# Spreading the gathers of mirrored rows over the steps, ordering the one-channel loads, and giving four side copies their own buffers

## The chip, the cores and the metric

The kernel runs on one core of a Trainium2 chip. The metric is device time of one execution in microseconds (us); smaller is better. Every quoted median is that of the fast runs of one kernel, with its lowest and highest run in brackets. Names of engines: PE is TensorE (matmuls), DVE is VectorE, ACT is ScalarE, POOL is GpSimd, SP is SyncE, whose queue issues most of the DMAs here.

## The reference

The input x has shape (8, 3008, 256) in float32: eight batches, a sequence of 3008 rows, 256 channels. The reference takes the real part of a two-dimensional Fourier transform, and feeds every row to a small network with an unusual activation.

```python
X = np.fft.fft(x, axis=1)            # over the 3008 rows
X = np.fft.fft(X, axis=2)            # over the 256 channels
x = X.real.reshape(8 * 3008, 256)
h = x @ w_in                          # 256 -> 2048
g = h * np.cos(h)
out = g @ w_out                       # 2048 -> 256
```

## The kernel before

The kernel uses the mirror symmetry of the transform, so that it handles 12032 columns instead of 24064 rows. It works in 47 tiles of 256 columns, each tile in 8 steps: 376 steps. A step is twenty 128x256 float32 matmuls, about 4.75 us of PE. Every step also asks four block sums of POOL (`sum_1` to `sum_4`), which feed matmuls into the accumulators pB, pC and pD.

Work for the next batch is scattered among these steps. POOL adds and subtracts rows with their mirror images ("folds", two halves of 1.0 us each); to this end, the rows must lie in four buffers `L[0]` to `L[3]`. The unmirrored ones come by plain DMAs from SP; the mirrored ones come by four indirect DMAs (gathers) that POOL issues itself:

```python
def load_x(b):
    L = [spool.tile([128, 6 * ND], FP, tag=f"xl{j}", bufs=1, name=f"xl{j}") for j in range(4)]
    for j in (2, 1):
        runs = (...)                               # two pieces of each row buffer
        for c, part in runs:
            nc.gpsimd.indirect_dma_start(          # not pinned: the scheduler places it
                out=L[j][:, part], out_offset=None, in_=xflat,
                in_offset=bass.IndirectOffsetOnAxis(ap=ix[:, c : c + 1], axis=0),
                element_offset=b * SEQ * ND,
            )
    for j, row in ((0, 0), (3, HALF)):
        nc.sync.dma_start(...)                     # plain loads
    ...
```

One channel (number 128) does not fit the symmetric layout of the channels. Its values are loaded for all batches at the start, one element at a time (four loads of 8 x 768 elements), stored to memory, read back in another layout by twelve small reads, folded by POOL, transformed by 28 matmuls, copied from PSUM by ACT ("side copies"), combined by DVE (first half) and POOL (second half), stored, and broadcast to the table `Rb`, which ACT needs for the third tile.

```python
def load_ext(j):                                   # called for j = 0..3
    ...
    with nc.allow_non_contiguous_dma(reason="one channel"):
        if j == 1:
            copy(0, 1, 0, 1)
            copy(1, 768, SEQ - 1, -1)
        else:
            copy(0, 768, (0, SEQ, HALF, HALF)[j], -1 if j == 2 else 1)
    nc.sync.dma_start(out=xe_dr[j], in_=t[:, 0:768])

def ext_side(g):                                   # called for g = 0..3
    par = g % 2
    t = spool.tile([128, 2 * NH], FP, tag=f"xt{par}", bufs=1, name=f"xt{par}")
    ...
    act(t[0:NB, 0:n], state["ext"][32 * g : 32 * g + NB, 0:n])
    state["side", par] = t[0:NB]
...
for b in range(1, NB):
    s0 = (b - 1) * steps_b                         # steps_b = 47
    l0 = s0 - (8 if b > 1 else 1.5)
    at(l0 * T + 0.1, lambda b=b: state.update(L=load_x(b)))
```

`at(t, fn)` sorts pieces of the program by a planned time, and `T` is one step. The plan fixes the program order. An instruction that is pinned (`pin`, which stands for `tc.keep_in_program_order`) keeps that order on its engine; one that is not may be moved by the scheduler.

## Time and profile before

| | before |
|---|---|
| time, median of 3 runs given with the kernel | 1990.61 us (1987.91 to 1991.32) |
| span of the profiled execution | 1993.1 us |
| PE busy | 1940.6 us, 97% |
| DVE, ACT, POOL busy | 71%, 73%, 68% |
| PE not busy | 52.5 us |

First lines of the page of before (span and busy time of PE and POOL), and from its list of groups the block sums of POOL (count, then busy time and mean ns of one, then idle time ahead of them and who ended it):

```profile
span 1993.1 us, 28143 instructions
PE 1940.6 (97%) x8855; PEld 1654.5 (83%) x8855; DVE 1417.0 (71%) x2343; ACT 1452.1 (73%) x2790; POOL 1352.9 (68%) x1860
L265 POOL TENSOR_TENSOR G<-G 128x256 f32<-128x256 f32 x1504 | 1079.7, 729 | 585.4 <-DVE G L705 490.0
```

PE is the bottleneck, and only its 52.5 idle microseconds can be won. POOL is idle for hundreds of microseconds, mostly waiting for DVE, and that costs nothing by itself. What counts is where POOL is late for PE. The view of waits of before shows what PE waits for (us in total, number of waits, longest):

```profile
PE pB L256 <- POOL G L265: 13.2, 14, 2.5
PE H L256 <- ACT H L268: 7.6, 5, 3.7
PE H L256 <- POOL xe L265: 7.5, 1, 7.5
```

The first line is POOL's lateness with block sums; the third is one wait for the one-channel data.

**The gathers.** POOL's timeline of before at the gathers of batch 3 (start, duration, what, and in brackets the idle time ahead of it):

```profile
408.20 3.03 POOL L265 TENSOR_TENSOR G<-G 128x256 f32<-128x256 f32 x4 [1.31 <-PE H L256]
411.19 0.99 POOL L315 TENSOR_TENSOR o<-xl 128x381 f32<-128x381 f32 x1
412.45 0.99 POOL L162 DMA_INDIRECT xl<-in_x_dram,ix  x1 [0.27 <-POOL o L315]
413.75 0.95 POOL L162 DMA_INDIRECT xl<-in_x_dram,ix  x1 [0.30 <-issue]
414.71 3.03 POOL L265 TENSOR_TENSOR G<-G 128x256 f32<-128x256 f32 x4
```

Between two sets of four sums there are a fold and two gathers, so this set of sums starts 6.5 us after the last, where a step has 4.75. PE's timeline of before shows what comes of it, here in batch 5:

```profile
895.06 0.59 PE L256 MATMUL pB<-G,w 128*128 128x256 f32 x2
897.11 0.70 PE L256 MATMUL pB<-G,WT 128*128 128x256 f32 x2 [1.46 <-POOL G L265]
897.64 1.03 PE L256 MATMUL H<-Ir,Ws 127*128 127x256 f32 x4
...
906.28 0.59 PE L256 MATMUL pB<-G,w 128*128 128x256 f32 x2
907.52 0.70 PE L256 MATMUL pB<-G,WT 128*128 128x256 f32 x2 [0.64 <-POOL G L265]
908.06 1.03 PE L256 MATMUL H<-Ir,Ws 127*128 127x256 f32 x4
```

Two waits of 1.46 and 0.64 us stand in this batch.

**The one-channel data.** The timeline of SP's queue in before. A DMA's "duration" here is how long its issue occupied the queue:

```profile
37.22 32.23 SPq L527 DMA_DIRECT2D x<-in_x_dram  x4
69.55 18.00 SPq L542 DMA_DIRECT2D xe_dr<-x  x3
87.60 0.68 SPq L527 DMA_DIRECT2D x<-in_x_dram  x1
88.34 10.06 SPq L548 DMA_DIRECT2D xs<-xe_dr  x1
```

The fourth big load is issued only at 87.60, behind three stores. Windows of 2 us of before show the hole that this leaves: the last two numbers of a line are the busy share of the DMA engines and the GB/s moved (ahead of them busy time and count of PE, PE's weight loads, DVE, ACT, POOL, then PE's granted clock).

```profile
84.00:86.00 2.00, 2.00 (x11) 1.74 (x11) 1.29 (x2) 1.49 (x3) 1.84 (x3) 1.00 0.31 19
86.00:88.00 2.00, 2.00 (x11) 1.76 (x10) 1.22 (x3) 1.97 (x5) 1.65 (x4) 1.00 0.00 0
```

The last of the twelve reads was issued by 108.4 us. POOL then folds, and PE goes on after its longest wait (POOL's line, then PE's, from their timelines in before):

```profile
110.50 0.38 POOL L265 TENSOR_TENSOR xs<-xs 128x96 f32<-128x96 f32 x1 [8.29 <-DMA out_dram<-ot]
```

```profile
111.30 4.18 PE L256 MATMUL H<-MC,xe 128*8 128x189 f32 x28 [7.48 <-POOL xe L265]
```

**The side copies.** ACT's timeline of before: the third and fourth copy wait for DVE, which still reads the two buffers that hold the first and second:

```profile
124.62 0.48 ACT L268 ACTIVATE xt<-H 8x378 f32<-8x378 f32 x1 [1.71 <-DVE ab L262]
125.72 0.48 ACT L268 ACTIVATE xt<-H 8x376 f32<-8x376 f32 x1 [0.62 <-DVE rx L262]
```

### The profile page before, as it was taken

The numbers are of one execution on the slowest core, as the hardware profiler recorded it, in microseconds if no ns is written. First come the engines' busy times: TensorE is split into PE (matmuls) and PEld (weight loads), VectorE is DVE, ScalarE is ACT, GpSimd is POOL, SyncE is SP. The second block draws the span as 40 slices with busy tenths as digits, with TensorE's granted clock in tenths as the row PEclk, the third lists the DMA queues.
The fourth block names the chain that finished last, engine by engine and source line by source line (L and its number), as shares of the span: only waits on it lengthen the run. The fifth ranks groups of instructions, "written<-read, shape, count | busy, mean of one in ns | idle before, by whom it ended". The sixth has DMA issues, their size and how long they took to land.

```text
span 1993.1 us, 28143 instructions
## 1 busy us (share of the span) xinstructions
PE 1940.6 (97%) x8855; PEld 1654.5 (83%) x8855; DVE 1417.0 (71%) x2343; ACT 1452.1 (73%) x2790; POOL 1352.9 (68%) x1860
## 2 busy tenths in 40 slices
PE   7979999999999999999999999999999999999997
PEld 4858888888888888888888888888888888888886
DVE  4757767777677767776677776777777776677776
ACT  2757767777777777777777777777777777777775
POOL 4758748786577866777667875778757776555654
PEclk9989999999999999999999999999999999999999
DMA  9822100121011110021100301013010110001101
GB/s 295 4 30 60 43 13 19 31 61 24 12 19 44 46 28 11 18 58 32 26 18 12 84 8 24 11 21 88 7 19 11 27 23 9 14 12 17 16 12 22
DMA packets 260207, 66.17 MB, mean 33 GB/s; under 512 B 247186, under 2 KB 250026, under 8 KB 260058
## 3 DMA queue, kind: packets, MB, share of 16 engines
q1 hardware_dynamic: 256362, 51.77, 15.0%
q0 software_dynamic: 3696, 12.60, 2.1%
q8 instruction: 70, 1.15, 0.2%
q14 instruction: 79, 0.65, 0.1%
HBM read 39.49 MB, written 24.80 MB: 32 GB/s over the span
## 4 chain that ended last, share of the span: by engine, by line
PE 82%; DMA 4%; DVE 4%; POOL 4%; ACT 2%; issue 2%; SPq 2%; DVEq 0%; POOLq 0%
PE H L256 33%; PE pC L256 14%; PE pB L256 14%; PE pD L256 14%; PE pA L256 7%; DMA x<-in_x_dram 2%; POOL G L265 2%; DVE G L705 1%; ACT G L268 1%; SPq L527 1%; DVE G L262 1%; DMA pick<-pick_mats 1%; POOL xl L162 1%; DVE v L262 1%; DMA xl<-in_x_dram 1%
## 5 line engine op out<-in xcount | busy, mean ns | idle before, releaser
L265 POOL TENSOR_TENSOR G<-G 128x256 f32<-128x256 f32 x1504 | 1079.7, 729 | 585.4 <-DVE G L705 490.0
L705 DVE SCALAR_TENSOR_TENSOR G<-H,G 128x512 f32<-128x512 f32 x376 | 257.0, 683 | 283.7 <-ACT G L268 283.7
L262 DVE TENSOR_TENSOR G<-H,G 128x512 f32<-128x512 f32 x376 | 260.0, 692 | 222.8 <-ACT G L268 219.7
L268 ACT ACTIVATE G<-H 128x512 int32<-128x512 f32 x376 | 224.5, 597 | 241.2 <-DVE G L262 239.8
L256 PE MATMUL H<-Rr,Wc 128*128 128x256 f32 x1504 | 387.9, 380 | 7.6 <-ACT H L268 7.6
L256 PE MATMUL H<-Ir,Ws 127*128 127x256 f32 x1504 | 388.6, 380 | 1.4 <-ACT E L268 1.4
L256 PE MATMUL pC<-G,WT 128*128 128x256 f32 x1504 | 387.3, 379 | 1.7 <-DVE u L262 1.6
L268 ACT ACTIVATE H<-Rb,wex 128x256 f32<-128x256 f32 x752 | 360.1, 479 | 34.1 <-DVE G L705 10.4
L268 ACT ACTIVATE E<-H 128x512 f32<-128x512 f32 x376 | 224.2, 596 | 216.7 <-PE H L256 214.0
L256 PEld LDWEIGHTS H<-Rr,Wc 128*128 128x128 f32 x1504 | 284.3, 190 | 56.5 <-ACT H L268 10.4
L256 PEld LDWEIGHTS pC<-G,WT 128*128 128x128 f32 x1504 | 284.1, 189 | 45.0 <-PE H L256 5.1
L256 PEld LDWEIGHTS H<-Ir,Ws 127*128 127x128 f32 x1504 | 283.4, 190 | 45.2 <-ACT E L268 6.6
L268 ACT ACTIVATE G<-G,halfpi 128x512 f32<-128x512 f32 x376 | 269.4, 716 | 1.5 <-DVE G L262 1.5
L262 DVE TENSOR_TENSOR G<-E,H 128x512 f32<-128x512 f32 x376 | 255.0, 678 | 12.6 <-PE H L256 10.4
L262 DVE TENSOR_TENSOR M<-G,M 128x512 f32<-128x512 f32 x376 | 257.6, 685 | 0.0
L705 DVE SCALAR_TENSOR_TENSOR G<-G,M 128x512 f32<-128x512 f32 x376 | 254.1, 676 | 0.4 <-ACT M L268 0.3
L268 ACT ACTIVATE M<-M,halfpi 128x512 f32<-128x512 f32 x376 | 246.1, 655 | 0.4 <-DVE M L262 0.3
L256 PE MATMUL pB<-G,WT 128*128 128x256 f32 x752 | 227.9, 385 | 13.2 <-POOL G L265 13.2
L256 PE MATMUL pA<-G,w 128*128 128x256 f32 x752 | 223.8, 379 | 2.3 <-issue 2.3
L268 ACT ACTIVATE M<-G 128x512 int32<-128x512 f32 x376 | 224.4, 597 | 0.0
L256 PE MATMUL pB<-G,w 128*128 128x256 f32 x752 | 223.7, 379 | 0.0
L256 PE MATMUL pD<-G,w 128*128 128x256 f32 x752 | 223.7, 379 | 0.0
(125 smaller groups left out, 1786.2 us busy)
## 6 DMA issues: line engine op xcount, KB each, us to landing
out_dram<-ot SPq DMA_DIRECT2D x504, 32.0 KB
xl<-in_x_dram SPq DMA_DIRECT2D x16, 512.0 KB
xl<-in_x_dram SPq DMA_DIRECT2D x32, 128.0 KB
out_dram<-ot SPq DMA_DIRECT2D x256, 2.0 KB
MC<-dft_mats SPq DMA_DIRECT2D x4, 943.5 KB
Rb<-r SPq DMA_DIRECT2D x10, 376.0 KB
w<-in_moe_w_in_dram SPq DMA_DIRECT2D x4, 512.0 KB
w<-in_moe_w_out_dram SPq DMA_DIRECT2D x1, 2048.0 KB
```

Of the source, the lines that this page charges most:

```text
L162: nc.gpsimd.indirect_dma_start(out=L[j][:, part], out_offset=None, in_=xflat, in_offset=bass.IndirectOffsetOnAxis(ap=ix[:, c : c + 1], axi ...
L256: nc.tensor.matmul(out_, lhsT=lhsT, rhs=rhs, start=start, stop=stop, skip_group_check=True)
L262: pin(nc.vector.tensor_tensor(out=o, in0=a, in1=b, op=op))
L265: pin(nc.gpsimd.tensor_tensor(out=o, in0=a, in1=b, op=op))
L268: pin(nc.scalar.activation(out=o, in_=i, func=func, **kw))
L527: nc.sync.dma_start(out=t[:, s0:s1], in_=bass.AP(tensor=xt, offset=x.offset + row * ND + 128, ap=[[SEQ * ND, NB], [step * ND, s1 - s0], [1 ...
L705: nc.vector.scalar_tensor_tensor(out=o, in0=h, scalar=TWO_PI, in1=c, op0=ALU.mult, op1=ALU.mult)
```

## The change

The change has three parts. The first takes POOL's gathers out of the crowded steps: for batches 2 to 7 they are pinned one per step, behind the four block sums, in steps that have no fold. Batch 1's four are pinned as well, which puts them later than the scheduler had put them, and the last rows of batch 7 go through SP's queue. The second pins all DMAs of the one-channel data in a fixed order: row 0 (a single element per batch) first, the four big loads, four stores, twelve reads. The third gives the four side copies four buffers. PE, DVE and ACT get exactly the same instructions in the same order as before; only POOL's and SP's orders change.

```diff
-    def load_x(b):
+    def gather_x(b, L, j, short):
+        ...                                  # the same slices and indices as before
+        pin(
+            nc.gpsimd.indirect_dma_start(
+                out=L[j][:, part], ...
+            )
+        )
+    GATHERS = [(2, 0), (2, 1), (1, 0), (1, 1)]
+    def load_x(b, gather=True):
...
-        if b == NB - 1:
-            nc.gpsimd.dma_start(out=L[1][0:1, 2 * ND : 5 * ND], ...)
+    def last_rows(b, L):
+        nc.sync.dma_start(out=L[1][0:1, 2 * ND : 5 * ND], ...)
...
+    def spin(**kw):
+        pin(nc.sync.dma_start(**kw))
+    def load_ext():
+            copy(1, 0, 1, 0, 1)              # row 0
+            copy(0, 0, 768, 0, 1)
+            copy(1, 1, 768, SEQ - 1, -1)
+            copy(2, 0, 768, HALF, -1)
+            copy(3, 0, 768, HALF, 1)
             for j in range(4):
+                spin(out=xe_dr[j], in_=rows[j][:, 0:768])
+            for j in range(4):               # three reads each
+                spin(out=xs[:, j, :, 0:4], ...)
...
-            [128, 2 * NH], FP, tag=f"xt{par}", bufs=1, name=f"xt{par}"
+            [128, 2 * NH], FP, tag=f"xt{par}", bufs=2, name=f"xt{par}"
-        state["side", par] = t[0:NB]
+        state["side", g] = t[0:NB]
...
-        at(l0 * T + 0.1, lambda b=b: state.update(L=load_x(b)))
+        at(l0 * T + 0.1, lambda b=b: state.update(L=load_x(b, b == 1)))
+        if b > 1:
+            for n, (j, short) in enumerate(GATHERS):
+                at((l0 + n) * T + 1.3, lambda ...: gather_x(b, state["L"], j, short))
+        if b == NB - 1:
+            at((l0 + 3) * T + 1.4, lambda b=b: last_rows(b, state["L"]))
```

More of the change, by code (lines that the diff above doesn't have):

```diff
@@ L148 @@
     nc.sync.dma_start(out=ix, in_=IX_dr.ap())
-    def load_x(b):
+    def gather_x(b, L, j, short):
+        if short:
+            c, part = 2 * j - 1, slice(0, 2 * ND)
+        else:
+            c = 4 if j == 1 and b == NB - 1 else 2 * j - 2
+            part = slice(2 * ND, 6 * ND)
+        pin(
+            nc.gpsimd.indirect_dma_start(
+                out=L[j][:, part],
+                out_offset=None,
+                in_=xflat,
+                in_offset=bass.IndirectOffsetOnAxis(ap=ix[:, c : c + 1], axis=0),
+                element_offset=b * SEQ * ND,
+            )
+        )
+    GATHERS = [(2, 0), (2, 1), (1, 0), (1, 1)]
+    def load_x(b, gather=True):
         L = [
@@ L154, in load_x @@
         ]
-        for j in (2, 1):
-            runs = (
-                (4 if j == 1 and b == NB - 1 else 2 * j - 2, slice(2 * ND, 6 * ND)),
-                (2 * j - 1, slice(0, 2 * ND)),
-            )
-            for c, part in runs:
-                nc.gpsimd.indirect_dma_start(
-                    out=L[j][:, part],
-                    out_offset=None,
-                    in_=xflat,
-                    in_offset=bass.IndirectOffsetOnAxis(ap=ix[:, c : c + 1], axis=0),
-                    element_offset=b * SEQ * ND,
-                )
+        if gather:
+            for j, short in GATHERS:
+                gather_x(b, L, j, short)
         for j, row in ((0, 0), (3, HALF)):
@@ L177, in load_x @@
                 )
-        if b == NB - 1:
-            nc.gpsimd.dma_start(
-                out=L[1][0:1, 2 * ND : 5 * ND], in_=xrows(b, SEQ - 3, 1, 1, 3)
-            )
-        return L
+        return L
+    def last_rows(b, L):
+        nc.sync.dma_start(
+            out=L[1][0:1, 2 * ND : 5 * ND], in_=xrows(b, SEQ - 3, 1, 1, 3)
+        )
     CC = cpool.tile([128, 512], FP, tag="CC")
@@ L518, in minus_sum, with copy @@
                 )
-    def load_ext(j):
-        if j == 0:
-            state["x1"] = spool.tile([128, HALF + 1], FP, tag="rx", bufs=1, name="x1")
-        t = state["x1"][j * NB : (j + 1) * NB]
-        def copy(s0, s1, row, step):
-            nc.sync.dma_start(
-                out=t[:, s0:s1],
+    def spin(**kw):
+        pin(nc.sync.dma_start(**kw))
+    def load_ext():
+        x1 = spool.tile([128, HALF + 1], FP, tag="rx", bufs=1, name="x1")
+        xs = state["xs"] = spool.tile([128, 4, NB, 6], FP, tag="xs", bufs=1, name="xs")
+        rows = [x1[j * NB : (j + 1) * NB] for j in range(4)]
+        def copy(j, s0, s1, row, step):
+            spin(
+                out=rows[j][:, s0:s1],
                 in_=bass.AP(
@@ L534, in copy @@
             )
-        with nc.allow_non_contiguous_dma(reason="one channel"):
-            if j == 1:
-                copy(0, 1, 0, 1)
-                copy(1, 768, SEQ - 1, -1)
-            else:
-                copy(0, 768, (0, SEQ, HALF, HALF)[j], -1 if j == 2 else 1)
-        nc.sync.dma_start(out=xe_dr[j], in_=t[:, 0:768])
-    def get_ext():
-        xs = state["xs"] = spool.tile([128, 4, NB, 6], FP, tag="xs", bufs=1, name="xs")
-        with nc.allow_non_contiguous_dma(reason="runs of six"):
+        with nc.allow_non_contiguous_dma(reason="one channel, then runs of rows"):
+            copy(1, 0, 1, 0, 1)
[3 more added lines that the diff above has]
+            copy(3, 0, 768, HALF, 1)
             for j in range(4):
-                nc.sync.dma_start(
+                spin(out=xe_dr[j], in_=rows[j][:, 0:768])
+            for j in range(4):
+                spin(
                     out=xs[:, j, :, 0:4],
@@ L553, in get_ext @@
                 for h in range(2):
-                    nc.sync.dma_start(
-                        out=xs[64 * h : 64 * h + 64, j, :, 4:6], in_=pairs[h]
-                    )
+                    spin(out=xs[64 * h : 64 * h + 64, j, :, 4:6], in_=pairs[h])
     def fold_ext():
@@ L600, in ext_rows @@
             state["rx"] = rx[0:NB]
-        rx, uv, b = state["rx"], state["side", 0], state["side", 1]
+        rx, uv, b = state["rx"], state["side", 2 * kodd], state["side", 2 * kodd + 1]
         a = spool.tile([128, NE], FP, tag="ab", bufs=2, name="ab")[0:NB]
@@ L1048 @@
         at(t, fn)
-    for j in range(4):
-        at(-T, lambda j=j: load_ext(j))
-    at(8 * T, get_ext)
-    at(11 * T + 1.35, fold_ext)
-    at(11 * T + 2.905, clear_ext)
-    at(11 * T + 4.75, dft_ext)
-    at(12 * T + 1.46, lambda: ext_side(0))
-    at(12 * T + 1.47, lambda: ext_side(1))
-    at(13 * T + 1.0, lambda: ext_rows(0, vtt))
-    at(13 * T + 1.46, lambda: ext_side(2))
-    at(13 * T + 1.47, lambda: ext_side(3))
-    at(14 * T + 1.35, lambda: ext_rows(1, gtt))
-    at(14 * T + 2.0, lambda: spread_ext(0, 1))
+    at(-T, load_ext)
+    e0 = 11 * T
+    at(e0 + 1.35, fold_ext)
+    at(e0 + 2.905, clear_ext)
+    at(e0 + 4.75, dft_ext)
+    for g in range(4):
+        at(e0 + T * (1 + g // 2) + 1.46, lambda g=g: ext_side(g))
+    at(e0 + 2 * T + 1.0, lambda: ext_rows(0, vtt))
+    at(e0 + 3 * T + 1.35, lambda: ext_rows(1, gtt))
+    at(e0 + 3 * T + 2.0, lambda: spread_ext(0, 1))
     fold_keys = [(k, p) for k in FOLDS for p in range(2 if k[0] not in "czx" else 1)]
@@ L1066 @@
         l0 = s0 - (8 if b > 1 else 1.5)
-        at(l0 * T + 0.1, lambda b=b: state.update(L=load_x(b)))
+        at(l0 * T + 0.1, lambda b=b: state.update(L=load_x(b, b == 1)))
+        if b > 1:
+            for n, (j, short) in enumerate(GATHERS):
+                at(
+                    (l0 + n) * T + 1.3,
+                    lambda b=b, j=j, short=short: gather_x(b, state["L"], j, short),
+                )
+        if b == NB - 1:
+            at((l0 + 3) * T + 1.4, lambda b=b: last_rows(b, state["L"]))
         f0 = max(7, s0 - 1)
```

## The prediction

> **What bounds the kernel.** TensorE: the page gives it 1940.6 of 1993.1 us busy (97%); DVE, ACT and POOL have 68 to 73%. The timeline shows steps of twenty 128x256 matmuls, one per 4.75 us, mostly without a gap. Only the 52 us of PE idle time can be won. Windows of 10 us place it: about 16 us in the start (before 57 us), 12 us between 103 and 141 us, about 10 us around the gathers of batches 2 to 7, most of the rest at the end.
>
> **Gathers.** In before, the scheduler lifts each batch's four gathers to just behind the last reads of the old rows, two and two, among steps that also carry a fold. A gather holds POOL for 0.96 us plus 0.30 us before it. Such a step has 3.03 us of block sums and 1.0 us of fold: 0.7 us is free against 2.5 us for two gathers. The PE timeline shows pB waiting for POOL: 0.81 (batch 2), 0.64+0.65, 1.06+0.66, 1.46+0.64, 0.81+0.66, and 0.53+2.46 in batch 7, where POOL also waits 1.14 us for a gather to land. Sum 10.4 us. In after, the instruction order has one gather per step, in steps without folds, behind the fourth sum, where POOL idles 1.3 us and more for DVE anyway. The last rows go over the sync queue. I expect all these waits gone: -10.4 us.
>
> **One-channel loads.** Each big one is 6144 single elements; from 46 to 82 us the DMA is 0.9 busy at 2 GB/s. This agrees with the Trainium skill (DMA: Bandwidth & Descriptors, Rules for kernel authors): a strided last dimension makes one descriptor per element. In before the fourth is issued only after three stores (87.6 us); windows of 2 us show the DMA idle from 84 to 89 us. It lands at 102.8; then one store, nine small reads (5.3 us of issues) and 1.7 us to landing at 110.2. After: the fourth follows at once and, I estimate, lands at 99 us; but all twelve reads (7.0 us) come after its store, so they land near 108.3. The PE stall before the one-channel matmuls (7.5 us) shrinks by about 2 us. Row 0 first changes nothing.
>
> **Side copies in own buffers.** ACT waits 1.71+0.62 us for DVE before copies 2 and 3. But DVE is busy with the rows until 125.69, where its next product now starts at 126.84: only 1.15 us is gained, as POOL's rows and the broadcast (PE waits at 136.8 and 141.0) follow this chain: -1.2 us.
>
> **Start.** Batch 1's gathers move behind the wex load and two weight sums; wex may land 1 to 3 us earlier, and PE's 3.7 us wait at 40 us shrink. That gains nothing: PE only reaches the wait for the DMA-bound one-channel data sooner. PE, DVE and ACT keep their order exactly.
>
> **Sum.** 1990.6 - 10.4 - 2.0 - 1.2 = 1977.0 us; range 1971 to 1983. Faster by over 2%: 0.01; within 2%: 0.98; slower by over 2%: 0.01.
>
> **What would show it.** Waits of pB for POOL gone from batches 2 to 7; no DMA hole near 86 us; POOL's wait for the one-channel data ending near 108 instead of 110.2; ACT's waits before the side copies gone, the broadcast landing 3 us before 139.9.
>
> **What would make it wrong.** Gathers that hold POOL longer at the new place, or delay the next sums; reads issuing slower than 0.6 us each; a start so late that it, not the DMA, ends the stall.

## The result, and the profile after

| | before | after |
|---|---|---|
| median (lowest to highest) | 1990.96 us (4 runs, 1987.91 to 1991.63) | 1973.76 us (4 runs, 1972.83 to 1977.76) |
| span of the profiled execution | 1993.1 us | 1971.4 us |
| PE busy | 1940.6 us | 1938.6 us |
| PE not busy | 52.5 us | 32.8 us |

The ratio is 0.992, with a 95% interval of 0.9903 to 0.9938: a little faster, within 2%. Ratios are computed as the mean time of one kernel's fast runs over that of the other's in the same rounds, so they are not quite the ratios of the medians. The medians differ by 17.2 us, where 13.6 was predicted. Over all rounds together, before ran 37 times with a median of 1990.91 us (1985.72 to 2001.78) and after 10 times with 1974.18 us (1972.83 to 1982.77), so 16.7 us apart.

The same lines of the page, for after:

```profile
span 1971.4 us, 28146 instructions
PE 1938.6 (98%) x8855; PEld 1654.3 (84%) x8855; DVE 1416.1 (72%) x2343; ACT 1452.0 (74%) x2790; POOL 1352.9 (69%) x1859
L274 POOL TENSOR_TENSOR G<-G 128x256 f32<-128x256 f32 x1504 | 1079.8, 728 | 571.8 <-DVE G L712 476.7
```

POOL does the same work in the same time; only its place has changed. PE's waits in after:

```profile
PE H L265 <- ACT H L277: 6.2, 4, 4.6
PE pB L265 <- POOL G L274: 3.0, 3, 1.8
```

The waits of pB for POOL fell from fourteen to three, the line with `POOL xe` is gone, and the longest wait for ACT, in the start, grew from 3.7 to 4.6 us. POOL's timeline of after, at the same gathers of batch 3:

```profile
485.55 3.02 POOL L274 TENSOR_TENSOR G<-G 128x256 f32<-128x256 f32 x4 [1.35 <-DVE G L712]
488.72 0.99 POOL L158 DMA_INDIRECT xl<-in_x_dram,ix  x1
491.81 3.03 POOL L274 TENSOR_TENSOR G<-G 128x256 f32<-128x256 f32 x4 [2.10 <-DVE G L712]
```

Between sums and gather lie 0.15 us now, and POOL still waits for DVE after the gather. SP's queue in after:

```profile
35.42 40.78 SPq L531 DMA_DIRECT2D x<-in_x_dram  x5
76.30 14.12 SPq L531 DMA_DIRECT2D xe_dr<-x  x4
90.47 7.73 SPq L531 DMA_DIRECT2D xs<-xe_dr  x12
```

The last read is issued by 98.2 us, ten earlier than in before. POOL folds without a wait, and ACT makes its third and fourth side copy without one (POOL's timeline of after, then ACT's):

```profile
105.36 0.39 POOL L274 TENSOR_TENSOR xs<-xs 128x96 f32<-128x96 f32 x1
```

```profile
115.86 0.98 ACT L277 ACTIVATE xt<-H 8x378 f32<-8x378 f32 x2
```

**A ruler for where the time went.** ACT copies one accumulator out at the end of each tile, so the time between two such copies is the length of a tile of eight steps. A clean tile takes 38.19 us in both kernels. Comparing tile by tile (worked out from ACT's timelines):

| stretch | before | after | saved |
|---|---|---|---|
| up to the copy of tile 0 | 90.79 | 93.99 | -3.20 |
| tile 0 to tile 1 (one-channel stage) | 56.59 | 45.14 | 11.45 |
| tile with gathers of batch 2 | 43.09 | 41.38 | 1.71 |
| batch 3 | 40.01 | 38.20 | 1.81 |
| batch 4 | 40.44 | 38.19 | 2.25 |
| batch 5 | 40.81 | 38.19 | 2.62 |
| batch 6 | 41.30 | 39.48 | 1.82 |
| batch 7 | 42.83 | 39.49 | 3.34 |

All other intervals between copies agree within 0.02 us. The six gather tiles sum to 13.55 us. The two profiled executions are 21.7 us apart, more than the medians: this table says what one pair of executions did, not what the change is worth. The first two rows and batch 7 differ most between executions of one program.

### The profile page after: what moved, and what is told of

It reads as the page before. It is cut to its first block, busy times and chain, and to the rows that moved or that the text cites. A ratio compares the mean times of both kernels' runs of the same rounds, so it can differ in the third digit from the quotient of the medians.

```text
span 1971.4 us, 28146 instructions
## 1 busy us (share of the span) xinstructions
PE 1938.6 (98%) x8855; PEld 1654.3 (84%) x8855; DVE 1416.1 (72%) x2343; ACT 1452.0 (74%) x2790; POOL 1352.9 (69%) x1859
## 3 DMA queue, kind: packets, MB, share of 16 engines
HBM read 39.49 MB, written 24.80 MB: 33 GB/s over the span
## 4 chain that ended last, share of the span: by engine, by line
PE 92%; DVE 3%; ACT 1%; issue 1%; DMA 1%; POOL 0%; SPq 0%; DVEq 0%; POOLq 0%; ACTq 0%
PE H L265 37%; PE pB L265 16%; PE pC L265 16%; PE pD L265 15%; PE pA L265 8%; DVE G L712 1%; DMA w<-in_moe_w_in_dram 1%; ACT G L277 1%; DVE G L271 0%; DVE v L271 0%; SPq L856 0%; DVE M L271 0%; ACT E L277 0%; POOL G L274 0%; DMA Rb<-r 0%
## 5 line engine op out<-in xcount | busy, mean ns | idle before, releaser
L277 ACT ACTIVATE H<-Rb,wex 128x256 f32<-128x256 f32 x752 | 360.2, 479 | 35.9 <-DVE G L712 10.4
L265 PE MATMUL pD<-G,WT 128*128 128x256 f32 x752 | 223.7, 379 | 0.0
```

The costliest lines, as they stand in the source:

```text
L265: nc.tensor.matmul(out_, lhsT=lhsT, rhs=rhs, start=start, stop=stop, skip_group_check=True)
L277: pin(nc.scalar.activation(out=o, in_=i, func=func, **kw))
```

## The experiments

Twelve runs were made, two of them (e1 and e10) of before and after themselves; all gave the right result. The first four ran on one chip together, e5 to e8 on a second and e9 to e12 on a third, each group beside 11 runs of before. "Timed" means the ratio to before with its 95% interval. The account that they test: the gathers give most of the gain; of the rest, does the order of the one-channel loads give anything, or do the shared buffers, or is it chance in the start?

### e1: before, looked at again

No edit.

> The kernel before, unchanged, profiled once more, to see what of the start and of the one-channel loads is chance. Theory A (the issue order makes the loads slow): the two middle loads take 13.5 to 14 us from one issue to the next again, the last alone 10 us; POOL waits for the one-channel data until about 110 us; PE idles about 7.5 us there. Theory B (the rate differs from run to run): one of these loads takes 10.5 to 11 us here, and the wait ends before 106 us. The start (first block sums on PE near 56.8 us in the first profile) may differ by up to 3 us under both.

Measured: 1996.47 us in a single run. PE waited 5.67 us for the one-channel data instead of 7.48, the interval from tile 0 to tile 1 was 54.17 us instead of 56.59, and the three single-element loads that can be timed by their issues took 14.7, 13.5 and 8.8 us where the first profile had 13.8, 13.5 and 10.1. The waits at the gathers came back, and one of them cost more than before: PE's timelines of before and then of e1, at the last wait of batch 7:

```profile
1388.02 0.70 PE L256 MATMUL pB<-G,WT 128*128 128x256 f32 x2 [2.46 <-POOL G L265]
1388.56 1.03 PE L256 MATMUL H<-Ir,Ws 127*128 127x256 f32 x4
```

```profile
1387.90 0.70 PE L256 MATMUL pB<-G,WT 128*128 128x256 f32 x2 [2.27 <-POOL G L265]
1388.43 1.56 PE L256 MATMUL H<-Ir,Ws 127*128 127x256 f32 x4
```

In e1 the granted clock fell to 0.50 for 3.41 us behind this wait; in before it stayed at 1.00. The tile took 44.34 us instead of 42.83. So the gathers' cost repeats, batch 7's with 1.5 us more; the one-channel stage does not repeat.

### e2: the gathers alone

Edit: part one of the diff above on the kernel before, nothing else.

> Before plus the gathers part alone (one pinned gather per step behind the sums, last rows on the sync queue). Theory (parts are independent, POOL's overrun is the cost): 1.7+1.8+2.2+2.6+1.8+3.3 = 13.5 us less, so a ratio of 0.9932, and no wait of pB for POOL in batches 2 to 7. Rival (the gain of the gathers was mostly that of batch 1's gathers at the start): start moves and less than 8 us in the later batches. If moving batch 1's gathers slows the start, the first steps come up to 3 us later, but the wait for the one-channel data absorbs that.

Measured: 1977.05 us (1973.57 to 1979.22, 6 runs), timed 0.9923 [0.9905, 0.9941]; before had 1991.27 (1987.96 to 1997.29). The tile intervals of batches 2 to 7 are those of after. Hence the gathers alone bring 14.2 us by the medians (15.7 by the means, from which the ratio is made), and nearly the whole of what the change brings.

### e3: the one-channel loads alone

Edit: part two of the diff on the kernel before.

> Before plus the one-channel loads in fixed order alone. Theory A (order alone): the big loads take 10.5 to 11.2 us from issue to issue, the data is there near 100 us, PE's 7.5 us wait is gone, and with it about 2 us at half clock behind it: 9 to 10 us less, ratio 0.9953. Theory of the prediction (only the hole in the DMA goes): data near 108 us, 2 us less, ratio 0.999. Rival (gathers of batch 1 out of the way made the loads fast): loads stay at 13.5 us.

Measured: 1994.02 us (1991.84 to 1999.30, 6 runs), timed 1.0014 [0.9995, 1.0033]: no gain. The profiled execution did lose the wait for the one-channel data, and the interval from tile 0 to tile 1 was 46.45 us instead of 56.59. But the copy of tile 0 came at 97.61 us instead of 90.79, so that two thirds of it was lost again in the start. Part of that lateness arose before any instruction that the edit moved (POOL issued the load that feeds wex at 28.53 us instead of 25.88), and in the start the granted clock was 0.50 for 10.24 and once more for 3.41 us, where before had 3.41 in all; so it is not shown to be the edit's doing. Why none of the six runs was faster than the median of before stays open.

### e4: the side copies alone

Edit: part three of the diff on the kernel before.

```diff
-            [128, 2 * NH], FP, tag=f"xt{par}", bufs=1, name=f"xt{par}"
+            [128, 2 * NH], FP, tag=f"xt{par}", bufs=2, name=f"xt{par}"
-        state["side", par] = t[0:NB]
+        state["side", g] = t[0:NB]
...                                          # and ext_rows reads them by g
```

> Before plus four own buffers for the side copies alone. Theory: 1.2 us less (DVE is busy with the rows until the side copies matter), ratio 0.9994, within noise; ACT no longer waits 1.7+0.6 us before copies 2 and 3; the broadcast lands 1 to 1.2 us sooner after the one-channel data than the 29.7 us of before (110.2 to 139.9). Rival (the whole ACT wait counts): 2.3 us.

Measured: 1988.92 us (1987.68 to 1989.48, 6 runs), timed 0.9985 [0.9969, 1.0001], which cannot be told from zero. The trace tells it better. Among all profiles without a stall of PE in front of the one-channel matmuls, the interval from tile 0 to tile 1 is 46.41 (e2) and 46.45 (e3) with shared buffers, and 45.05 to 45.28 with own ones (after, e4, e6 to e11). The difference is 1.3 us. Note that e4 had no stall either, with the old order of loads and the hole: the hole is not enough to cause the stall.

### e5: batch 1's gathers back at their early place

Edit, on after:

```diff
-        pin(
+        (pin if b != 1 else lambda ins: ins)(
```

> After, with batch 1's four gathers alone left to the scheduler, which puts them where before had them (ahead of the wex load). Theory (the moved gathers delay the start): from the issue of the wex load to the first H on ACT 7.3 to 7.9 us as in the four profiles with this place, not 8.5 to 9.7 us as in the two with the new place; the start 1 to 2 us earlier, and about 1.5 us less than after in all, as no later wait absorbs it. Rival (the start differs by chance): no difference between the two.

Measured: six runs at 1970.84, 1972.41, 1972.62, 1973.45, 1983.75 and 1983.87 us, median 1973.04, timed 0.9922 [0.99, 0.9944], beside 1990.91 (1985.72 to 1994.13) for before. Two groups. The profiled execution was the 1983.87 one. In it the loads took 15.4, 14.1 and 13.8 us, the last read was issued at 112.8, and PE stalled for 8.41 us with after's order of loads. The interval from tile 0 to tile 1 was 55.74 us, 10.6 more than after's 45.14, which is about the distance of the two groups. So the new order of loads does not prevent the stall, and one execution with a stall costs 10 to 11 us. That the other slow run stalled too is likely, but only one execution is profiled.

### e6: keeping PE busy in the start with one-row matmuls

After's PE waits 4.64 us for ACT at 37 to 42 us, and its granted clock then is 0.66 on average from 40 to 50 us. The question was whether that lowered clock costs time that filler matmuls can win back. Edit, on after, behind the second half of the first transform:

```diff
+    filler = bank("pB")
+    for _ in range(12):
+        mm(filler, zero[:, 0:128], zero[:, 0:1].to_broadcast([1, 512]), True)
```

> After plus twelve 1x512 filler matmuls between the last matmul of the I transform and the first H, where PE waits 3.6 to 5.9 us for ACT. Theory (that idle time halves the granted clock, and the half clock costs): no clock of 0.5 in the 6 to 10 us behind the wait, the 19 matmuls there faster, the start 1.5 to 2.5 us earlier; if the fillers end before ACT's H they delay nothing. Rival (DVE and ACT set the pace there): clock at 1.0, but the start no earlier.

Measured: 1974.94 us (1974.20 to 1975.05, 5 runs), timed 0.9922 [0.9906, 0.9938]: as after. PE's timeline of e6 shows the fillers and what came next:

```profile
37.59 3.29 PE L265 MATMUL pB<-zero 1*128 1x512 bf16 x12
44.31 2.07 PE L265 MATMUL H<-Rr,Wc 128*128 128x256 f32 x4 [3.43 <-ACT H L277]
```

Four such matmuls take 1.13 us at full clock behind a short wait; here they took 2.07. The windows show the granted clock at 0.50 already from 40 to 41 us, while the fillers ran: these matmuls of one row did not hold the clock.

### e7: two gathers per step

Edit, on after:

```diff
-                    (l0 + n) * T + 1.3,
+                    (l0 + n // 2 * 2) * T + 1.3,
```

> After with two gathers in one step, in the same steps without folds. POOL's step is then 3.03+2.52 = 5.6 us against 4.75. Theory A (one gather per step is what counts): two waits of pB for POOL in each of batches 2 to 7, 6 to 12 us more than after. Theory B (the fold in the same step is what counts; POOL runs 0.9 us ahead and takes up 0.8 us): within 3 us of after.

Measured: 1975.63 us (1973.74 to 1976.30, 5 runs), timed 0.9926 [0.991, 0.9942], and all intervals of batches 2 to 7 equal to after's. Two gathers in one step cost nothing where that step has no fold.

### e8: one gather per step, in steps with folds

Edit, on after: the first step of the gathers, `l0`, is moved to the one behind the last fold that reads the old rows, so that the four gathers fall among the folds.

```diff
-        l0 = s0 - (8 if b > 1 else 1.5)
+        l0 = (step behind the fold "o1" of the previous batch) if b > 1 else s0 - 1.5
-                    (l0 + n) * T + 1.3,
+                    (l0 + n) * T + 1.35,
```

> After with one gather per step, but in the steps right behind the last reads of the old rows, most of which hold a fold too: 3.03+1.0+1.26 = 5.3 us of POOL against 4.75. Theory A (one per step is enough): as after. Theory B (POOL's budget of a step counts): the overruns of 0.5 us add up over the four steps, less 0.9 us that POOL is ahead: about 1 us for each of batches 2 to 7, 4 to 8 us more than after, with waits of pB for POOL in these batches.

Measured: 1975.43 us (1974.16 to 1977.26, 5 runs), timed 0.9928 [0.9911, 0.9944], again with all intervals equal to after's. One gather beside a fold costs nothing either. POOL's timeline of e8, at the gathers of batch 3:

```profile
414.72 3.03 POOL L274 TENSOR_TENSOR G<-G 128x256 f32<-128x256 f32 x4 [0.77 <-DVE G L712]
...
417.77 1.00 POOL L324 TENSOR_TENSOR o<-o,o 128x381 f32<-128x381 f32 x1
418.92 0.99 POOL L158 DMA_INDIRECT xl<-in_x_dram,ix  x1
419.93 3.03 POOL L274 TENSOR_TENSOR G<-G 128x256 f32<-128x256 f32 x4
...
424.50 3.04 POOL L274 TENSOR_TENSOR G<-G 128x256 f32<-128x256 f32 x4 [0.43 <-DVE G L712]
```

The step with fold and gather takes POOL 5.21 us (414.72 to 419.93), more than the 4.75 of a step. But the next one has no fold, and POOL waits for DVE again behind it: it has caught up. In batch 2 all four gathers stand beside a fold; three such steps in a row take 5.21, 5.28 and 5.11 us, 1.35 us too much together, and still PE does not wait. Together e7 and e8 say that either separation, of the gathers from the folds or of the gathers from each other, would have been enough.

### e9 and e10: after without the loads, and after again

Edit of e9, on after: part two of the diff is undone (before's `load_ext` and `get_ext`); e10 is after itself, on the same chip.

> After without the change of the one-channel loads (gathers and side copies only). Theory (that part is worth little in the mean, as the loads' speed differs by chance and is mostly enough): within 2 us of after, measured in the same rounds. Rival (the fixed order takes away the stalls that before's order has when the loads are slow): 3 us or more above after, with single runs 5 to 10 us above the others.

> After, unchanged, for its spread on the chip of the other three: 1972 to 1978 us, ratio 0.992. Big loads anywhere from 9 to 15 us each; PE idle before the one-channel matmuls only if they are slow.

Measured: e9 1974.73 us (1972.40 to 1978.60, 6 runs), timed 0.992 [0.9892, 0.9947]; e10 1974.75 us (1972.96 to 1982.77, 6 runs), timed 0.9925 [0.9895, 0.9954]; before 1990.24 (1986.33 to 2001.78). The loads' part shows no gain in the mean. In e9's profile the last read was issued by 102.3 us and PE did not stall.

### e11: filler matmuls of full height

Edit, on after, at the place of e6's:

```diff
+    for _ in range(5):
+        mm(filler, CC[:, 0:128], CC, True)
```

> After plus five 128x512 fp32 filler matmuls of full 128 rows (4.7 us) in the wait at about 38 us; the 1-row fillers of the earlier run let the clock fall to 0.5 while they ran. Theory (the clock follows the work in the array, and the half clock costs): clock 1.0 from 36 to 52 us, the first steps 1.5 to 3 us sooner after ACT's first H, and 1.5 to 3 us less than after. Rival (the pace there is DVE's and ACT's): clock 1.0, less than 1 us gained.

Measured: 1973.96 us (1972.55 to 1976.51, 6 runs), timed 0.9916 [0.9889, 0.9942]. These fillers held the clock: PE's timeline of e11 has the same four matmuls at 1.13 us, and the windows show a granted clock of 1.00 from 36 to 64 us. (They differ from e6's in height, type and length at once, so which of these counts is not told apart.)

```profile
38.60 4.45 PE L265 MATMUL pB<-CC 128*128 128x512 f32 x10
44.62 1.13 PE L265 MATMUL H<-Rr,Wc 128*128 128x256 f32 x4 [1.56 <-ACT H L277]
```

From there to the first matmul of the steps into pA went 15.2 us, where after took 18.2, e10 18.9, and e6 and e8, whose first such matmuls came as late as e11's, 17.6; so the half clock cost 2.4 to 3.7 us of the start. But PE's wait for ACT happened to end 2.8 us later in this execution than in after's (44.62 against 41.80), which ate nearly all of it, and six runs do not resolve what remains.

### e12: e5's edit and four fillers together

Edit, on after:

```diff
-        pin(
+        (pin if b != 1 else lambda ins: ins)(
+    filler = bank("pB")
+    for _ in range(4):
+        mm(filler, CC[:, 0:128], CC, True)
```

> After with batch 1's gathers in before's place and four such fillers (3.7 us). Theory: both gains add, 3 to 4 us less than after in the runs whose one-channel loads are in time, 1969 to 1971 us; runs with slow loads lose up to 10 us of it again, since the earlier start only meets the wait sooner.

Measured: 1970.43, 1970.79, 1972.76, 1973.41, 1978.52 and 1981.27 us, median 1973.08, timed 0.9912 [0.9882, 0.9942]. The profiled execution (1978.52) stalled 6.29 us. Its best runs are the fastest, but the mean is not told apart from after's. No version was shown to beat after.

### All fourteen profiles together

| place of batch 1's gathers | profiles | PE stalled before the one-channel matmuls | last read issued by (us) | wex: issue to first use (us) |
|---|---|---|---|---|
| early (before, e1, e3, e4, e5, e12) | 6 | 4: 7.48, 5.67, 8.41, 6.29 us | 99.3 to 112.8 | 7.1 to 7.9 |
| late (after, e2, e6 to e11) | 8 | 0 | 98.2 to 105.8 | 8.0 to 10.7 |

Three of the big single-element loads can be timed by their issues; one took anything from 8.7 to 15.4 us. Much of this is chance: before, e1 and e4 have the same program up to there, and their three took 37.4, 37.0 and 30.6 us together; likewise after, e10, e7 and e8, with 32.3, 31.9, 35.0 and 38.0 us. The new order of issues does not go with fast loads: e5 has it and took 43.3, e9 has the old one and took 32.0. Four stalls of six against none of eight suggests that the early gathers, which move rows while the first of these loads start, have a part in it. It is not shown: the gathers were not moved alone with enough profiled executions.

## Why the prediction was right, point by point

**The total.** 1977.0 was predicted, 1973.76 measured, within the range of 1971 to 1983; "within 2%" was right. The gain was 17.2 us by the medians against 13.6. That the sum came this close is in part luck: the loads' 2.0 us, which did not appear, made up for part of what the gathers' term was short.

**The gathers: right in mechanism, short in size.** The waits went as said, and e2 shows the gain by itself. The term was -10.4 and measured -13.55 in the pair of profiles, -15.2 to -15.3 in the three other profiles with before's gathers. The prediction added up the idle times that the timeline shows. Take the first wait of batch 5 above. The pairs into pB start at 895.06 and 897.11, 2.05 us apart, where undisturbed pairs start 0.43 us apart: 1.62 us are lost, though only 1.46 are shown as idle, as a pair is recorded 0.59 us long and so overlaps the next by 0.16. The matmuls behind the wait start 0.53 us on instead of 0.43: another 0.10. So 1.46 of idle time cost 1.72, and each such wait costs 0.26 more than it shows. The batch has two: (1.46 + 0.26) + (0.64 + 0.26) = 2.62, which is what the tile interval lost. The Trainium skill (Perfetto Trace Analysis, Tensor Engine Instruction) says that the end of a PE record is estimated and thus a model; this trace agrees, with records of 0.59 us that follow one another every 0.43. The prediction also overlooked one wait of 0.54 us in batch 2. All twelve waits show 10.92 us; with 12 x 0.26 that makes 14.04. In batches 3, 4 and 5 this sum is exact to 0.01 us; in 2, 6 and 7 it is 0.17 too high each, a remainder not traced. And 13.55 is the lowest value of four: in e1, e3 and e4, which have before's gathers too, the last wait of batch 7 (2.27 to 2.55 us) put the granted clock at 0.50 for 3.41 us, as in e1's lines above. Batch 7's tile took 44.34 to 44.56 us there, and the six tiles together 15.2 to 15.3 us more than in after.

**Why the waits arose: the budget of a step was too strict.** The prediction named both parts of the new place, one gather per step and steps without folds, as the cure. e7 and e8 show that either suffices. By its own numbers (0.7 us free beside sums and fold, 1.26 us for a gather), even one gather beside a fold would be late. It is not: a pinned gather costs 0.15 + 0.99 us, not every step has a fold, and even the 1.35 us too much of three such steps in a row (e8, batch 2) do not reach PE. What made POOL late for PE at these places in before was a fold and two gathers in one step, 6.5 us; in batch 7 POOL also waited 1.14 us, for a gather to land, ahead of the load of the last rows.

**The one-channel loads: the hole went, the gain did not appear.** The prediction estimated the fourth load to land at 99 us and the reads near 108.3. In after's profile, the stores behind the loads had been issued by 90.4 and the last read by 98.2, and the stall was gone altogether; the broadcast landed at 131.7 instead of 139.9, where 3 us were predicted. Yet e3 (1.0014) and e9 beside e10 (medians 1974.73 and 1974.75) show no gain in the mean. The step that failed is "shrinks by about 2 us": it took the load times of one execution (13.8, 13.5, 10.1 us) as fixed. They range from 8.7 to 15.4, in part by chance, and where the last read was issued by 105.8 us or earlier, PE did not stall, whichever the order; where it was issued at 107.6 or later, it did. That each load is this slow for so few bytes agrees with the Trainium skill (DMA: Bandwidth & Descriptors, Rules for kernel authors), by which a strided last dimension becomes one descriptor per element: the DMA engines were 0.9 busy at 3 to 4 GB/s from 60 to 80 us. "Row 0 first changes nothing" had no run of its own.

**The side copies: right.** -1.2 predicted; 1.3 us by the intervals without a stall, and both waits of ACT are gone.

**The start: wrong in its sign.** "wex may land 1 to 3 us earlier" was the step. wex is the column form of one weight row; ACT needs it for its first H. Its issue on POOL and the first use on ACT, in before (POOL's timeline, then ACT's):

```profile
31.59 1.23 POOL L288 DMA_DIRECT2D wex<-wx  x1 [0.66 <-DMA wx<-Ws]
```

```profile
38.89 0.99 ACT L268 ACTIVATE H<-Rb,wex 128x256 f32<-128x256 f32 x2 [6.82 <-DMA wex<-wx]
```

In after, again POOL's and ACT's timelines:

```profile
32.30 1.22 POOL L297 DMA_DIRECT2D wex<-wx  x1 [4.96 <-DMA wx<-Ws]
```

```profile
40.76 0.99 ACT L277 ACTIVATE H<-Rb,wex 128x256 f32<-128x256 f32 x2 [8.27 <-DMA wex<-wx]
```

POOL was free earlier and waited 4.96 us instead of 0.66, since the issue waits for the row to land, not for POOL. And from issue to first use went 8.46 us instead of 7.30; over all profiles 8.0 to 10.7 with the gathers late against 7.1 to 7.9 with them early. Why the load itself is slower then is open. No stall follows in after that would absorb the later start; but what it costs in the whole run is not shown, as the ratios to before of e5 (0.9922) and of after (0.992) are not told apart.

The wait of PE behind it brings the half clock, which the prediction did not price. The Trainium skill (TensorE: Matmul & The Clock Gate, Part 1) says that an idle window of about 3.4 us brings the clock to 4/8, that about 3.4 us of sustained activity releases it, and that these windows run free of the kernel. The traces agree with the windows: in each profile every stretch of granted clock 0.50 starts on one grid of 3.41 us, whose phase differs between executions, and lasts 3.41, 6.83 or 10.24 us (only the one at the end of the program has other lengths). They differ in the idle window, which need not be wholly idle. We added up PE's gaps of over 0.15 us window by window, without the first 25 and the last 15 us. The clock fell at the end of windows with about 2 us of idle time or more (1.99 us in e3 was enough, 2.00 us in before was not), with e6's fillers as the one exception; it came back at the end of windows with at most 0.52 us, and with 0.69 us or more it stayed at 0.50. So what a wait of 2 us or a little more costs depends on where the grid lies: before's 2.46 us in batch 7 fell across two windows (0.95 and 1.51 us) and cost no clock, e1's 2.27 us fell in one. This chance is part of why the start differs between executions of one program.

**What remains.** Gathers and side copies make 14.9 of 17.2 us (16.7 over all runs) by the pair of profiles, and by estimate 16.5 to 16.6 with the gathers' 15.2 to 15.3 of the other three. So little is left to explain. Fewer stalls of about 10 us and a start later by 1 to 3 us may stand against each other in it; that is argued from the profiles, not shown.

## What to carry to other kernels

When a helper engine has time to spare on average, look at the single step in which several of its jobs fall together: here a fold and two gathers at once cost PE 13.55 us in twelve waits, or 1.7 us more where one of them also halved the clock, and it was enough to take either the fold or one of the gathers out of that step. Measure such a loss by the distance between equal marks of the pacing engine, not by the idle time in its records, which was a fifth short here. And before pricing the order of slow small DMAs from one trace, look at a second execution of the same kernel: what differs between two runs of one program is no property of the order.

## What the Trainium skill lacked or had wrong

- **Perfetto Trace Analysis** says that PE's end times are a model, but not what follows for waits: the idle time shown before a matmul understates the loss. Here the difference was 0.16 us of overlapping records and 0.10 us of slower restart at each wait, 10.92 us shown and 13.55 lost.
- **TensorE: Matmul & The Clock Gate** speaks of an idle window of about 3.4 us and warns of gaps of over about 3 us. Here waits of 2.27 to 2.55 us already brought the clock to 0.50 in e1, e3 and e4, where about 2 us or more of them fell in one window of the grid (1.99 to 2.27 us), and no figure of the page says how much idle time a busy window may hold: 0.52 us still released the clock, 0.69 us did not.
- The same page does not say that matmuls of one row may not count as activity: twelve of them (3.29 us) let the clock fall to 0.50 while they ran, five matmuls of full height in float32 (4.45 us) kept it at 1.00; they differ in type and length as well.
- **DMA: Bandwidth & Descriptors** has the rule of one descriptor per element, but no time for descriptors of one element and no warning of its spread: a load of 8 x 768 single elements took 8.7 to 15.4 us and kept the issuing queue occupied for as long; three of them took 30.6 to 37.4 us together in executions of the same program.
- No page gives the time for which POOL itself is held by an indirect gather, during which it does no other work: 0.95 to 0.99 us in the steps shown here, with 0.15 to 0.30 us ahead of it. Perfetto Trace Analysis says only that the record of such a DMA ends when its descriptors are generated, and DMA: Bandwidth & Descriptors gives a time to the first byte, not the time that POOL is held.
